# One kernel, two lists of orders and engines: attention by landmarks and a feed-forward block on one core

## The chip, the core and the metric

The kernel runs on one core of a Trainium2 chip. That core has a tensor engine for matmuls (PE, with its weight loads shown apart as PEld), a vector engine (DVE), an activation engine (ACT), a general engine (POOL) and a sync engine that only issues transfers (SP). Each takes its instructions in its own order; an instruction starts when what it reads is written and what it overwrites is no longer read. The metric is the device time of one execution in microseconds (us).

## The reference

Eight batches of eight heads, 576 positions and 64 columns a head. The attention replaces a 576x576 softmax by three small ones over 32 landmarks, with an iterated inverse between them; a feed-forward block with a residual follows, over rows of 512.

```python
def _attn_ref(q, k, v):                            # q, k, v: 8 x 8 x 576 x 64
    q_lm = q.reshape(B, H, m, S // m, D).mean(axis=3)   # m = 32 landmarks
    k_lm = k.reshape(B, H, m, S // m, D).mean(axis=3)
    A  = sm(q, k_lm)                               # sm: softmax(scale * a b^T)
    Bm = sm(q_lm, k_lm)
    C  = sm(q_lm, k)
    Z = Bm^T / (norm1(Bm) * norm_inf(Bm) + 1e-06)
    for _ in range(6):
        Z = 2 * Z - Z @ Bm @ Z
    return A @ Z @ C @ v

def _moe_ref(x, g_ln, w_ch1, w_ch2):               # x: 8 x 576 x 512
    xn = (x - mean(x)) / sqrt(var(x) + 1e-06) * g_ln
    ch = maximum(xn @ w_ch1, 0.0) @ w_ch2          # 512 -> 2048 -> 512
    return x + ch
```

## The kernel before

**Operations and buffers.** The kernel first defines 1571 operations by name. Each has a body of one or some instructions, the engines that may run it, and the buffers that it uses; nothing is issued yet. `ORDER`, a string near the top, is then gone through: `38P` is operation 38 on PE, `D`, `A`, `G` and `S` stand for DVE, ACT, POOL and SP. `emit` (L174) calls the body on the named engine, and every instruction keeps its place in program order. So the string sets, for each engine, the sequence of its instructions, and it sets buffers too: at the first use of a buffer in the string `emit` takes the first free slot of its kind, and with the last use the slot goes back to the end of the free list. The kinds have few slots: two double banks of PSUM (`p2`, for psh, psm, pst and others), four single ones (`bank`), six staging tiles for loads from memory (`stg`), two for v of the later batches (`vs`), eleven blocks of rows (`xblk`). No planner runs; the string is all that sets the order.

**Start.** `constants` (L250 to L289) fills zeros, identities and masks. Two loads of q, two of k, one of g and two of v are issued on SP, then eight loads of w1 (512 KB each, L345) as `stg` slots come free, and four of w2 on POOL. PE runs `warm` groups meanwhile (L309): matmuls of zeros into an idle bank, which nobody reads, one group of 24 with 160 columns and fourteen of 4 with 128 columns.

**First batch** (`def_batch0`, L531). q and k are cast to fp16 (`cast`), PE turns their tiles (pst, L197) and sums them over segments of 18 positions (pss, with pm); `qbd` and `klm` are the landmarks' sums. From these come three exponentials: `it` (32x32, for Bm), `ect` (for C) and `ea` (for A; `psd`, `lns` and `norm` divide it by its sums). `softmax`, `gram`, `scaled` and six `step`/`next` pairs are the iterated inverse: a step is 8 small matmuls it<-st on PE, next is st<-st,it on DVE (L210). `product` is C times v (pscv), `cv` its scaled copy, `pszt`/`zt` and `pszc`/`zcbd` the products of the inverse with cv, which the feed-forward block takes.

**Later sets** (`def_set`, L676). Batches 1, 2 and 3, 4 and 5, 6 and 7 go through the same steps, in wider tiles, between the matmuls of the batches ahead of them. Here the landmark sums come from DVE, POOL or PE, and the turned tiles from DVE.

**Feed-forward of a batch** (`def_rows` L965, `def_measure` L989, `def_first` L1015, `def_block` L1091, `def_seven` L1130). `rows` makes x<-psy, the attention's output in rows; `measure` its mean and variance (DVE). w1 is scaled by g (`scale_w1`, L357) and its mean over rows taken off (`less`: psf, then less<-psf). `psm` multiplies zt with w1 (16 small-tile matmuls), `m16` copies it to fp16, `psh` multiplies that with ea: sixteen blocks a batch, each of 4 matmuls of 288 columns into a `p2` slot. `relu` (L1068 on DVE, L203 on ACT) empties it into hT. pso multiplies hT with w2 (16 matmuls of 512 columns for 128 rows). From the third batch on, four of the row blocks are made by seven products instead of eight (`def_seven`: ps7a, ps7c, ps7e), which needs sums of hT (`hmix`, 1024 columns) and differences of w2 (`mix`). `done`/`add7` add to x on DVE, `store` writes it, on SP or ACT.

Of the kernel before, what the change touches and what calls it, by code (L numbers as in the profile page):

```python
# [19 lines left out]
0G 20P 23P 4S 12P 14P 24P 17P 11P 2S 1S 3S 6S 7S 10P 21P 28G 38P 25A 26D 34P 39D 40P 29P 30A 31P 27D  # L20
37P 32P 42D 41D 18P 33D 43P 65P 44A 45D 66A 61P 67P 46P 47P 250G 48D 22P 19P 15P 62A 68A 69A 71D
245G 49P 50D 63P 35P 13P 79G 80D 51P 52D 64A 36A 81P 70D 53P 72P 73A 5S 95S 54D 8P 9D 105A 106G 55P
56D 57P 74P 82D 260P 83D 58D 16P 84D 96S 59P 75A 76A 60D 85P 251D 86D 89P 90D 87P 88D 126P 261A 262D
108G 77G 94S 103G 93S 97S 101G 91D 92D 78D 107A 102G 127P 128P 129P 130A 167P 141P 142A 252P 253A
145P 169D 104A 168D 98S 254D 149P 150D 147P 148A 172P 173A 176P 247P 177A 248A 259D 255D 174P 175A
246D 256P 257A 146A 170P 171D 109G 110G 121P 122P 123P 111G 124P 268P 156P 258D 151D 249D 267P 112A
125A 275A 269A 270A 271A 157D 277A 158D 131P 132P 133P 134P 178P 163P 278D 279D 117G 273A 433G 274A
99S 113G 135A 180D 263S 164A 159P 280P 281D 160A 165P 166A 114G 264A 100S 115G 116G 265S 118G 136P
137P 266G 161P 179D 429G 119G 138P 139P 162D 282P 283D 140A 181P 182A 183P 284P 276D 285A 143P 187P
184D 286P 144A 188A 272D 152D 185P 186A 287D 297P 298D 299D 189P 191D 190D 288P 289A 294P 290P 295A  # L30
201P 202P 296A 300P 301A 291D 292P 293A 120G 455G 212P 213P 435G 436G 437G 310P 438G 445G 302A 303G
308P 309A 214P 330P 434D 444D 312D 311D 313D 332D 192P 193A 153D 154D 198P 199A 155A 441D 430D 439D
431D 331D 442D 440D 432D 443D 234P 556D 215P 304P 235P 236P 305A 306A 196P 446G 447G 203P 204P 194P
195A 237P 238P 205P 206P 451G 197A 307G 314P 315A 337P 339P 448G 449D 822G 338A 555D 239P 240P 241P
322P 207P 208P 574D 565D 569G 450D 340A 323A 216P 242D 209D 210S 217P 324D 341P 343D 223P 335P 244S
336A 342D 333P 463D 218P 219P 577G 452D 220D 344P 352P 353D 467G 468G 469G 470G 334A 826G 348P 345A
349A 346P 347A 457G 318P 319A 224P 316P 317A 225P 226P 227P 481P 458G 465D 459G 460G 482A 350P 454D
354D 357P 471D 464D 472D 351A 453D 363P 228P 229P 364D 358A 361P 230P 362A 461D 462D 365D 493P 494A
359P 368P 360A 483P 495P 355P 325D 326D 505A 369A 356A 231D 233A 200G 374P 375P 366P 367A 370P 371A
573G 506D 456D 507P 508P 509D 320P 321D 385P 484P 486A 487A 489A 510P 834D 511D 466D 491A 386P 387P  # L40
485A 388P 211S 512P 376P 473S 474G 490A 377P 496P 498A 501A 499A 497A 513D 514P 327D 488D 492D 328D
396P 397P 475S 476G 566G 828G 829G 830G 831G 572G 477S 478G 838G 839G 844G 564G 568G 503A 378P 379P
380P 515D 823D 502A 221S 504D 372P 516P 479S 480A 500D 517D 836D 528P 529P 530D 531D 398P 399P 373A
381P 522P 518P 389P 329A 866S 382D 418P 519D 824D 559D 520P 521D 523A 532P 419P 420P 524A 533A 534A
# [1219 lines left out]
```

## Time and profile before

| what | value |
| --- | --- |
| device time, median of 3 runs | 260.54 us (260.16 to 260.61) |
| span of the profiled execution, first to last instruction | 258.5 us |
| the median less that span | 2.0 us |
| instructions in the span | 8351 |
| busy: PE / DVE / POOL / ACT | 249.9 / 212.3 / 177.5 / 163.9 us |
| granted clock of PE, mean | 1.000 |
| moved by DMA | 36.32 MB, 140 GB/s |

The span and the busy times are those of one profiled execution; the device time also holds what lies before the first and behind the last instruction. A row of a timeline gives the start in us, the time in us, the engine, the line, the operation with what it writes and reads, its tile and shape, how many in a row (x4), and in brackets the idle time of the engine ahead of it and what ended it. The time of a row of matmuls runs from the start of the first to the end of the last, and ends overlap with the next row's start. A row of a table by stage gives the stretch, its length, the busy time of PE, PEld, DVE, ACT and POOL with the count of instructions, the granted clock, the busy share of the DMA engines and GB/s.

### The profile page before, as it was taken

What the parts mean: (1) busy time and instruction counts of PE and PEld (TensorE: products, weight loads), DVE (VectorE), ACT (ScalarE), POOL (GpSimd) and SP (SyncE); (2) the same over time, 40 slices, a digit from 0 to 9 for tenths busy, and PEclk for the clock granted to TensorE, in tenths of its full rate; (3) what the DMA queues carried; (4) which work ended last, traced back from release to release, by engine and by line L of the source; (5) the groups of instructions that cost most, each with busy time, mean ns of one, the idle gap of its engine ahead of it and who ended that gap; (6) DMA issues with size and microseconds to landing.
All of it is one profiled execution on the core that took longest, in us unless ns stands there. A gap on an engine that the chain in (4) does not pass through costs nothing.

```text
span 258.5 us, 8351 instructions
## 1 busy us (share of the span) xinstructions
PE 249.9 (97%) x3499; PEld 179.8 (70%) x3499; DVE 212.3 (82%) x472; ACT 163.9 (63%) x304; POOL 177.5 (69%) x180
## 2 busy tenths in 40 slices
PE   7898999999999999999999999999999999999993
PEld 7766465556554557777766787777867787788981
DVE  1669899999999989997998869898547999878661
ACT  1588886747766999778756997868666245644000
POOL 8324899689794789699999995782078505966600
PEclk9999999999999999999999999999999999999999
DMA  6999999999749176949704832500130100510356
GB/s 234 367 269 338 374 210 208 207 235 244 227 127 178 29 164 87 221 89 286 140 4 121 231 93 61 127 3 3 41 85 0 44 20 9 115 23 20 82 121 184
DMA packets 23277, 36.32 MB, mean 140 GB/s; under 512 B 2116, under 2 KB 11592, under 8 KB 23240
## 3 DMA queue, kind: packets, MB, share of 16 engines
q1 hardware_dynamic: 12456, 23.37, 29.6%
q0 software_dynamic: 9504, 10.36, 25.1%
q10 hardware_dynamic: 1280, 2.07, 3.1%
q8 instruction: 27, 0.44, 0.7%
q14 instruction: 10, 0.08, 0.1%
HBM read 36.70 MB, written 9.44 MB: 178 GB/s over the span
## 4 chain that ended last, share of the span: by engine, by line
PE 85%; DMA 7%; ACT 3%; DVE 2%; issue 1%; SPq 1%; ACTq 0%; DVEq 0%
PE psh L193 23%; PE ps7a L193 16%; PE pso L193 15%; PE ps7c L193 8%; DMA w1s<-in_moe_w_ch_dram 5%; PE ps7e L193 4%; PE psm L193 3%; PE psy L193 3%; DMA stg_q<-in_q_dram 3%; PE it L193 2%; PE pscv L193 2%; PE psd L193 1%; PE psec L193 1%; PE psea L193 1%; PE pso_74a L193 1%
## 5 line engine op out<-in xcount | busy, mean ns | idle before, releaser
L203 ACT ACTIVATE hT<-psh 128x576 f16<-128x576 f32 x106 | 65.8, 650 | 30.4 <-PE psh L193 28.6
L193 PEld LDWEIGHTS <-hT 128*128 128x128 f16 x688 | 64.6, 98 | 22.6 <-issue 3.1
L193 PE MATMUL psh<-ea,m 128*128 128x288 f16 x512 | 78.2, 286 | 0.1
L193 PEld LDWEIGHTS <-m 128*128 128x128 f16 x512 | 48.9, 98 | 15.6 <-issue 1.3
L193 PE MATMUL pso<-w,hT 128*128 128x512 f16 x176 | 45.5, 380 | 0.0
L207 POOL TENSOR_TENSOR mix<-hT 128x1024 f16<-128x1024 f16 x8 | 17.0, 2125 | 27.4 <-ACT hT L203 27.4
L210 DVE SCALAR_TENSOR_TENSOR x<-ps7a,rstd,x 128x256 f32<-128x256 f32 x48 | 21.3, 477 | 6.7 <-PE ps7a L193 4.9
L193 PE MATMUL ps7a<-mix,hT 128*128 128x256 f16 x192 | 25.9, 273 | 0.0
L1068 DVE TENSOR_SCALAR hT<-psh 128x576 f16<-128x576 f32 x22 | 16.4, 753 | 10.1 <-PE psh L193 9.9
L997 DVE BATCH_NORM_STATS2 six<-x 128x6 f32<-128x512 f32 x36 | 24.2, 673 | 0.0
L207 POOL TENSOR_TENSOR ea<-ea,lns 128x576 f16<-128x576 f16 (+1 forms) x14 | 17.7, 1261 | 7.2 <-ACT lns L203 4.0
L200 ACT CAST m<-psm 128x512 f16<-128x512 f32 (+1 forms) x25 | 19.1, 793 | 4.5 <-PE psm L193 3.4
L200 ACT COPY x<-psy 128x512 f32<-128x512 f32 (+1 forms) x29 | 16.8, 587 | 7.6 <-PE psy L193 7.2
L193 PEld LDWEIGHTS <-mix 128*128 128x128 f16 x192 | 18.2, 98 | 4.3 <-issue 1.5
L207 POOL TENSOR_TENSOR mix<-mix,hT 128x1024 f16<-128x1024 f16 x8 | 16.9, 2124 | 6.2 <-DVE mix L207 5.8
L207 POOL TENSOR_TENSOR hT<-hT 128x1024 f16<-128x1024 f16 x9 | 19.1, 2123 | 0.2
L207 POOL TENSOR_TENSOR hT<-hT,mix 128x1024 f16<-128x1024 f16 x7 | 15.1, 2166 | 4.4 <-PE ps7e L193 2.5
L214 DVE TENSOR_REDUCE part<-xT_k 128x32 f16<-128x576 f16 x24 | 17.1, 737 | 0.0
L207 POOL TENSOR_TENSOR asum_q<-asum_q 128x256 f32<-128x256 f32 (+1 forms) x24 | 15.1, 628 | 1.5
L203 ACT ACTIVATE ec<-psec 128x256 f16<-128x256 f32 (+1 forms) x42 | 12.4, 428 | 5.3 <-PE psec L193 5.3
L193 PE MATMUL psy<-zcbd,ea 128*128 128x256 f16 x80 | 14.8, 273 | 0.2 <-ACT x L200 0.2
L200 POOL CAST natv<-stg_v 128x1152 f16<-128x1152 f32 (+1 forms) x12 | 13.8, 1163 | 1.4 <-DMA stg_v<-in_v_dram 1.3
(174 smaller groups left out, 471.2 us busy)
## 6 DMA issues: line engine op xcount, KB each, us to landing
out_dram<-x SPq DMA_DIRECT2D x55, 128.0 KB, 2.7
stg_v<-in_v_dram SPq DMA_DIRECT2D x10, 576.0 KB, 5.1
w1s<-in_moe_w_ch_dram SPq DMA_DIRECT2D x8, 512.0 KB, 11.6
nat_q<-in_q_dram POOLq DMA_DIRECT2D x7, 576.0 KB, 8.7
nat_k<-in_k_dram POOLq DMA_DIRECT2D x7, 576.0 KB, 7.5
w<-in_moe_w_ch_dram POOLq DMA_DIRECT2D x4, 512.0 KB, 8.5
out_dram<-x ACTq DMA_DIRECT2D x15, 128.0 KB, 2.4
stg_v<-in_v_dram SPq DMA_DIRECT2D x6, 288.0 KB, 4.5
```

What stands on the lines that cost most here:

```text
L193: keep(nc.tensor.matmul(o, l, r, start=start, stop=stop, tile_position=(rb, cb), skip_group_check=(skip or cb != 0)))
L200: keep(nc.scalar.copy(o, i) if e == "A" else ENGINES[e].tensor_copy(out=o, in_=i))
L203: keep(nc.scalar.activation(*args, **kw))
L207: keep(ENGINES[e].tensor_tensor(out=o, in0=a, in1=b, op=f))
L210: keep(ENGINES[e].scalar_tensor_tensor(out=o, in0=a, scalar=s, in1=b, op0=f0, op1=f1))
L214: keep(nc.vector.tensor_reduce(out=o, in_=i, axis=axis, op=f))
L997: keep(nc.vector.bn_stats(out=T(f"six_{j}")[:], in_=T(f"x_{j}")[:]))
L1068: keep(nc.vector.tensor_scalar(out=o, in0=T(psh)[:, :, 0:HS], scalar1=0.0, scalar2=None, op0=ALU.max))
```

## The change

Only `ORDER` is different. The same 1571 operations stand in it with the same buffers; their sequence is another from the first row on, and 139 have another engine. The rest of the kernel is the same, line by line.

```diff
 ORDER = """
-0G 20P 23P 4S 12P 14P 24P 17P 11P 2S 1S 3S 6S 7S 10P 21P 28G 38P 25A 26D 34P 39D 40P 29P 30A 31P 27D
-37P 32P 42D 41D 18P 33D 43P 65P 44A 45D 66A 61P 67P 46P 47P 250G 48D 22P 19P 15P 62A 68A 69A 71D
...
+4S 0G 13P 12P 18P 17P 15P 24P 28G 5S 23P 14P 21P 250G 11P 20P 2S 26D 19P 16P 10P 38P 40P 39A 22P 34P
+1S 25D 42A 8P 3S 27D 32P 33D 7S 80G 31P 245G 29P 30A 37P 41D 43P 44A 65P 66A 61P 45D 67P 6S 62A 47P
...
```

Of the operations with another engine: 18 `relu` go from DVE to ACT and 12 from ACT to DVE; of the x copies 10 go from ACT to DVE and 6 back; of `m16` 8 from ACT to DVE and 7 back; of `hmix` 9 from DVE to POOL and 8 back; of `mix` 4 from DVE to POOL and 5 back; of the stores 16 from SP to ACT and 5 back, 2 from ACT to POOL and 1 from SP to POOL. Both half `norm`s of the first batch's first unit go from DVE to POOL. The `cast_v` of the first batch's second unit goes from DVE to POOL, where that of the first unit is already; three later ones go from ACT to POOL and two back. The rest are single small casts, copies and scalings, in both directions. By operations: ACT has 316 instead of 311, DVE 399 instead of 398, POOL 159 instead of 153, SP 75 instead of 87, PE 622 as before.

Rows of an engine's sequence show what stands there now; an order row gives line, operation, what it writes and reads, and the shape, without any time.

First place: PE, where the `warm` groups end and the first transposes of k (pst_k) begin. Before:

```order
L193 MATMUL idle<-zeros 128x128
L193 LDWEIGHTS zeros
L193 MATMUL idle<-zeros 128x128
L197 LDWEIGHTS nat_k
L197 MATMUL pst_k<-ident_64,nat_k 128x128
```

And now:

```order
L193 MATMUL idle<-zeros 128x160
L193 LDWEIGHTS zeros
L193 MATMUL idle<-zeros 128x160
L197 LDWEIGHTS nat_k
L197 MATMUL pst_k<-ident_64,nat_k 128x128
```

Before, 56 idle matmuls stand ahead of pst_k (seven groups of 4, the one of 24, one of 4), and six groups of 4 follow between later work. Now 76 stand ahead (thirteen groups of 4, then the one of 24), and one group of 4 is left for later.

Second place: DVE, right behind `scaled` of the first batch (st<-it,cinv) and up to both cv; the last `next` (st<-st,it of 128x2x32) follows the second cv in both lists. Here st<-st,it stands for a `next`, ea<-ea,lns for half a `norm`, natv for `cast_v`, cv for the scaled product. Before:

```order
L207 TENSOR_TENSOR ea<-ea,lns 128x288
L210 SCALAR_TENSOR_TENSOR st<-st,it 128x128
L200 CAST natv_76<-stg_v 128x2x9x64
L210 SCALAR_TENSOR_TENSOR st<-st,it 128x128
L207 TENSOR_TENSOR ea<-ea,lns 128x288
L210 SCALAR_TENSOR_TENSOR st<-st,it 128x128
L1202 TENSOR_SCALAR g_sb<-psg 128x4
L210 SCALAR_TENSOR_TENSOR st<-st,it 128x128
L217 RECIPROCAL rcv<-pscv 128x2
L633 TENSOR_SCALAR cv<-pscv,rcv,cinv 128x130
L210 SCALAR_TENSOR_TENSOR st<-st,it 128x128
L633 TENSOR_SCALAR cv<-pscv,rcv,cinv 128x130
```

And now:

```order
L200 COPY xT_q<-pst_q 128x1152
L210 SCALAR_TENSOR_TENSOR st<-st,it 128x128 x3
L1202 TENSOR_SCALAR g_sb<-psg 128x4
L217 RECIPROCAL rcv<-pscv 128x2
L210 SCALAR_TENSOR_TENSOR st<-st,it 128x128 x2
L633 TENSOR_SCALAR cv<-pscv,rcv,cinv 128x130 x2
L210 SCALAR_TENSOR_TENSOR st<-st,it 128x2x32
L207 TENSOR_TENSOR ea<-ea,lns 128x288
```

The cast of v and two half norms are gone from DVE here (the half norm behind the last `next` is one of the second unit), a copy of xT_q (on ACT before) stands ahead of the first `next`, and both cv stand ahead of the last one.

Third place: ACT from the second scaling of w1 (w<-w1s,g_sb) to the first wide evictions of the first batch (hT<-psh) and the last scaling. Before:

```order
L203 ACTIVATE w_16_78<-w1s,g_sb 128x512
L200 CAST less<-psf 128x512
L200 COPY x<-psy 128x512
L200 CAST tot_q<-psl_q 128x128
L203 ACTIVATE w_16_78<-w1s,g_sb 128x512
L200 COPY x<-psy 128x512
L203 ACTIVATE hT<-psh 128x576 x2
L200 CAST tot_k<-psl_k 128x128
L203 ACTIVATE hT<-psh 128x576
L200 CAST tot_k<-psl_k 128x128
L200 COPY x<-psy 128x512
L203 ACTIVATE w_16_78<-w1s,g_sb 128x512
```

And now:

```order
L200 CAST zt<-pszt 128x2x32
L203 ACTIVATE w_16_78<-w1s,g_sb 128x512
L200 CAST less<-psf 128x512
L200 COPY x<-psy 128x512
L200 COPY x<-psy 64x512
L200 COPY x<-psy 128x512 x2
L203 ACTIVATE hT<-psh 128x576 x2
L203 ACTIVATE w_16_78<-w1s,g_sb 128x512
L203 ACTIVATE hT<-psh 128x576 x2
L200 CAST less<-psf 128x512
L203 ACTIVATE w_16_78<-w1s,g_sb 128x512
```

The four small casts (tot_q, tot_k) are gone to DVE, a copy of zt and the 64-row copy of x have come from DVE, and the second cast of less stands ahead of the scaling that follows it.

166 lines of the change are left out of this document (83 added, 83 removed).

## The prediction

> **What bounds the kernel now.** I read the page's first section and its chain first, then the busy time by stage, then PE's rows of the first 24 us, then what DVE and ACT do up to 42 us.
>
> ```profile
> span 258.5 us, 8351 instructions
> PE 249.9 (97%) x3499; PEld 179.8 (70%) x3499; DVE 212.3 (82%) x472; ACT 163.9 (63%) x304; POOL 177.5 (69%) x180
> PE 85%; DMA 7%; ACT 3%; DVE 2%; issue 1%; SPq 1%; ACTq 0%; DVEq 0%
> ```
>
> PE is busy for 97% of the span and holds 85% of the chain that ended last. DVE, at 82%, is the next. The stages (columns: stretch, length, then busy time of PE, PEld, DVE, ACT, POOL) say where PE is not full:
>
> ```profile
> 0.00:7.50 7.50, 6.10 (x57) 6.10 (x58) 1.84 (x9) 1.28 (x1) 6.29 (x29) 1.00 0.72 258
> 7.50:23.50 16.00, 13.90 (x321) 10.19 (x319) 11.96 (x36) 11.98 (x19) 4.69 (x6) 1.00 1.10 307
> 23.50:42.30 18.80, 18.18 (x280) 11.03 (x278) 17.32 (x41) 15.74 (x35) 16.07 (x22) 1.00 1.15 290
> 42.30:254.20 211.90, 211.75 (x2849) 152.50 (x2848) 180.57 (x388) 134.93 (x250) 150.49 (x124) 1.00 0.49 111
> 254.20:258.50 4.30, 0.00 (x0) 0.00 (x0) 0.61 (x1) 0.00 (x0) 0.00 (x0) 1.00 0.46 132
> ```
>
> From 42.3 to 254.2 us PE rests 0.15 us of 211.90. There the list can only lose, or arrange PE's own work better. What a list can gain or lose by waits lies in the first 42.3 us: 7.5 us of idle matmuls and data on the way, then 16.00 - 13.90 = 2.1 and 18.80 - 18.18 = 0.6 us without a matmul, and some more that the busy time hides, as it counts each matmul to the end of its latency. The last 4.3 us are one DVE operation and its stores.
>
> PE's own work has a price for the order. In the chain of waits (start, us, what), four matmuls of one kind take longer where a small-tile matmul stands next to them:
>
> ```profile
> 113.58 0.44 PE ps7c L193 x4
> 117.25 0.49 PE psh L193 x4
> 118.06 0.60 PE psh L193 x4
> 118.65 0.65 PE psm L193 x16
> 119.52 0.54 PE ps7a L193 x4
> ```
>
> A psh block costs 0.49 us beside its like and 0.60 before psm; a ps7 block 0.44 beside its like and 0.54 behind the small steps. So each excursion from 128*128 tiles to small ones costs 0.10 us of PE.
>
> **The change part by part.** It adds and removes no operation. By rows the engines' sums stay: 18 evictions hT<-psh go from DVE to ACT and 12 come back, 9 mixes go from DVE to POOL and 8 back, and so on; no engine's total moves by more than a few us, and none is PE's. I make the sum over six terms, against the profiled execution (span 258.5; the median of the runs, 260.54, lies 2.0 above it, and that 2.0 is kept).
>
> *One, the idle matmuls ahead of the first transposes.* Today 7 short groups (4 matmuls of 128 columns), the long one (24 of 160) and one short group run there, and six short ones fill later gaps. In the new list 13 short groups and the long one come first, and one is left for later.
>
> The rows of PE's list shown with the change have the long group last, with pst_k right behind it. PE's rows of the trace, with the idle time before each in brackets:
>
> ```profile
> 1.40 6.26 PE L193 MATMUL idle<-zeros 128*128 128x128 f16 x56 [1.40 <-DVE zeros L252]
> 7.50 0.67 PE L197 MATMUL pst_k<-ident,nat_k 128*128 128x128 f16 x9
> 9.12 0.68 PE L197 MATMUL pst_q<-ident,nat_q 128*128 128x128 f16 x9 [0.44 <-ACT nat_q L200]
> 10.24 0.44 PE L193 MATMUL pss_q<-pm,nat_q 128*128 128x64 f16 x9 [0.18 <-DVE nat_q L200]
> 10.51 0.67 PE L197 MATMUL pst_k<-ident,nat_k 128*128 128x128 f16 x9
> 11.02 0.39 PE L193 MATMUL idle<-zeros 128*128 128x128 f16 x4
> 13.11 0.84 PE L193 MATMUL idle<-zeros 128*128 128x128 f16 x12
> ```
>
> Eight more such matmuls make 0.84 of 0.39, so one costs 0.056 us there. Five more groups are 20 matmuls, 1.1 us: pst_k begins at 8.6, not 7.5. Today PE then waits for q (0.44 and 0.18 us), and the last q sums start at 10.24. From 8.6 the new list runs two transposes of k (0.51 each by 10.51 to 11.02), one of q, four sums (0.27 each by 10.24 to 10.51), a filler and turn_g with no wait, as all of q has landed by then (DVE casts its last part from 9.42): the last sums end at 11.6 against 10.5, and qbd, which reads them, is 1.0 late.
>
> The Trainium skill, "TensorE: Matmul & The Clock Gate", Part 1, says that PE starts at half rate and goes to the full one after a busy window of about 3.4 us that runs free of the kernel, so that the moment varies between runs. The trace agrees with the two rates (56 matmuls with 6.26 us to their end, and 0.056 us for one later). By that rule this term stays 1.1 us, since the added groups run after the change of rate either way. The same section lets the rate fall again after an idle window of that length; in the new list no rest of PE comes near it.
>
> *Two, the first batch's chain (softmax, Gram, six steps).* It is a chain from PE to DVE and back. Rows of its steps and of what DVE and ACT do between:
>
> ```profile
> 13.98 0.24 PE L193 MATMUL it<-st 32*32 32x64 f16 x8
> 17.18 0.24 PE L193 MATMUL it<-st 32*32 32x64 f16 x8
> 17.82 0.24 PE L193 MATMUL it<-st 32*32 32x64 f16 x8 [0.40 <-DVE st L210]
> 19.14 0.22 PE L193 MATMUL it<-st 32*32 32x32 f16 x8
> 19.69 0.21 PE L193 MATMUL pszt<-st,cv 32*32 32x32 f16 x8 [0.33 <-DVE st L210]
> 9.84 1.12 ACT L200 COPY xT_q<-pst_q 128x1152 f16<-128x1152 f16 x1 [0.77 <-PE pst_q L197]
> 15.06 0.76 DVE L200 CAST natv<-stg_v 128x1152 f16<-128x1152 f32 x1
> 17.88 0.41 DVE L633 TENSOR_SCALAR cv<-pscv,rcv,cinv 128x130 f16<-128x130 f32 x1
> 23.48 1.14 PE L193 MATMUL psh<-ea,m 128*128 128x288 f16 x8
> ```
>
> Bare, a step takes 0.64 us (17.18 to 17.82); today five take 5.16 (13.98 to 19.14), with a cast of v (0.76) and two half norms on DVE, three fillers and other matmuls in between. In the new list the cast and the norms are gone to POOL (DVE's rows are shown with the change; st<-st,it is what follows a step). One copy stands there ahead of the first st<-st,it, and the two cv ahead of the last. The new first step comes at 15.4: 1.0 late from qbd, and 0.4 more because the ACT copy of xT_q (1.12, now from 11.4) and the q transposes of the second unit stand ahead of it on ACT and PE. Then 0.76 (the copy), 0.64, 0.9 (product_0, 0.7, in between), 0.7 and 0.7 lead to the sixth at 19.1: level with 19.14. The two cv push pszt to 20.0 (+0.3). Behind it ACT's scaling of w (0.72) comes after ztc_00 there, so the mean of w is 0.7 late, psm and the two m16 evictions more, and the first psh starts at 24.7 against 23.48, with one 0.22 matmul pair more done: 1.0 late.
>
> *Three, 23.5 to 42.3.* DVE is 17.32 us busy of 18.80 here and ACT 15.74. The rows to convert:
>
> ```profile
> L1068 DVE TENSOR_SCALAR hT<-psh 128x576 f16<-128x576 f32 x3 | 2.3, 756 | 0.4 <-PE psh L193 0.4
> L203 ACT ACTIVATE hT<-psh 128x576 f16<-128x576 f32 x11 | 6.8, 651 | 1.8 <-PE psh L193 1.6
> L203 ACT ACTIVATE w<-w1s,g_sb 128x512 f16<-128x512 f32 x4 | 2.9, 720 | 0.9 <-DMA w1s<-in_moe_w_ch_dram 0.9
> L200 DVE COPY x<-psy 64x512 f32<-64x512 f32 x1 | 0.7, 694 | 0.0
> 31.54 1.19 ACT L203 ACTIVATE hT<-psh 128x576 f16<-128x576 f32 x2 [0.33 <-PE psh L193]
> 33.47 1.16 ACT L200 CAST natv<-stg_v 128x1152 f16<-128x1152 f32 x1
> 15.84 11.95 DMA w1s<-in_moe_w_ch_dram
> 42.33 0.41 PE L193 MATMUL psm<-w,zt 64*32 64x512 f16 x8
> ```
>
> All three psh evictions (2.3) and the 64-row x copy (0.7) leave DVE, two small casts come: about 15 of 18.80 remain. ACT takes the three (each 0.54 behind its like, as 1.19 for two says), the copy and one w scaling, and gives the cast of v (1.16) to POOL and two lns passes to later: about 16. The late engine, DVE, gets 2.3 us of air. Also less_0 moves ahead of the scaling that waits for the w1 part that lands last (15.84 + 11.95 = 27.8), which it stands behind today. Walking the new list with these durations, ACT's run of evictions sets PE's pace from 30 us (psh_001, 008, 009 and 011 each wait for the eviction two blocks back), the first step of the next set comes out at 33.7 (34.08 today, with 0.7 us more of PE's other work done by then), and psm_10 starts at 41.5. Today it starts at 42.33 with two pso matmuls and one psd pair (0.68) more done. At equal work that is -0.15: the 1.0 is won back. Bounds: nothing won back, +1.0; with 0.8 lost to ACT on top, +1.8; all of DVE's lateness gone, -1.8.
>
> *Four, PE's arrangement.* I count 61 excursions to small tiles today, 55 in the new list; 45 and 39 after psm_10. Six by 0.10 are -0.6; as some of the merged neighbours change shape still, I take -0.4 (bounds -0.6 and 0).
>
> *Five, covers after 42.3.* DVE, ACT and POOL must still deliver before PE asks. The thinnest I found: psec_11 needs the banks of psec_10, which ACT empties.
>
> ```profile
> 68.97 0.70 PE L193 MATMUL psec<-xT_k,lm 32*32 32x288 f16 x32
> 69.71 1.72 ACT L203 ACTIVATE ec<-psec 128x256 f16<-128x256 f32 x6 [1.00 <-PE psec L193]
> L207 POOL TENSOR_TENSOR hT<-hT,mix 128x1024 f16<-128x1024 f16 x7 | 15.1, 2166 | 4.4 <-PE ps7e L193 2.5 <-DVE mix L207 1.9
> ```
>
> The six ec end 2.46 us after psec starts; the new list has psec, the Gram matmuls, three pso pairs and a step between (2.55). It holds by 0.1. In the last batch three POOL mixes in a row (6.4) stand under 16 seven-blocks (7.2). Taken 0; bounds 0 and +2.1, one POOL mix uncovered.
>
> *Six, loads, stores and the end.* The w1, v and w2 loads keep their order up to a swap of neighbours, and each is wanted later than it lands today. Nine stores more go to ACT's queue, which rests 37% of the span. The last matmuls, done_74a and its two stores are the same: 0.
>
> Sum: -0.15 - 0.4 = -0.55, so 257.9 of span and 260.0 us.
>
> **The rivals.** *ACT takes DVE's place as the late engine* (slower). From the first wide block on, every second psh waits for ACT. For it: in the stretch ACT's list carries twelve psh evictions, five copies of x and three scalings of w, and PE waits for the eviction two blocks back at four places of my walk. Against: 16 of 18.8 is less than DVE's 17.3. Price: +1.0 and +0.8, less 0.4: 261.9. *DVE's lateness vanishes* (faster): the start's delay is hidden because DMA sets w1's pace anyway, and 1.8 is won before 42 us: 258.3. For it: DVE's 92%; against: ACT's run. *An uncovered POOL mix late in the program*: +2.1 - 0.55, 262.1; against it the 0.8 us of spare. *The rate of PE falls* between 11 and 20 us, as only one filler is left: a window of 3.4 us by the skill's page would cost half of it, 1.7; by rows, PE's idle share there is 2.1 of 16 and its longest rest 0.44. The price by rows is some 30 PE operations at twice their time, +1.5: 261.5.
>
> **How the numbers follow.** Forecast 260.0 with 40% (its own range 259.2 to 260.9), ACT 24%, DVE 25%, POOL 8%, rate 3%. A measurement tells about 0.2% (0.52 us) from no change. Of the forecast's 40, 20 lie below 260.02, 17 within and 3 above; DVE gives 23 and 2; ACT 3 within and 21 above; POOL 2 and 6; rate 3 above. Faster 43%, same 24%, slower 33%. The range runs from 257.5 to 263.0.
>
> **What would show it.** Right: pst_k near 8.6, the first psh near 24.7, psm_10 near 41.5, PE resting under 0.5 us after it. Wrong: psm_10 beyond 43 with ACT evictions named before PE's waits (ACT); before 40.5 (DVE); a rest of PE over 1 us after 42 named by POOL or DVE mixes (POOL).

## The result, and the profile after

The new list is slower: 262.65 us (median of four runs) against 260.58, a ratio of 1.008 (95% interval 1.0064 to 1.0096). Ratios here and below leave out slow runs, over 1.5% above the fastest of the same kernel, as one of the four is (266.48). I had forecast 260.0, a little faster. Timed again beside other kernels (e8 below) the ratio was 1.013 (1.010 to 1.016), so the loss is between 2 and 3.5 us.

The page of the profiled execution of the new list, its span, busy times and shares of the chain:

```profile
span 260.8 us, 8339 instructions
PE 250.6 (96%) x3499; PEld 179.7 (69%) x3499; DVE 213.0 (82%) x473; ACT 161.3 (62%) x300; POOL 182.5 (70%) x186
PE 88%; DVE 1%; issue 0%; ACT 0%
```

The span is 2.3 longer, 260.8 against 258.5; PE is busy 0.7 longer and idle 1.6 longer. By stage (the columns as in the prediction, with the granted clock third from the end):

```profile
0.00:7.50 7.50, 6.10 (x78) 6.10 (x79) 1.08 (x8) 1.28 (x1) 5.85 (x29) 1.00 0.70 239
7.50:23.50 16.00, 13.18 (x275) 8.75 (x272) 9.75 (x29) 9.32 (x15) 7.61 (x10) 0.79 1.09 325
23.50:42.30 18.80, 18.14 (x270) 11.27 (x269) 16.20 (x42) 16.58 (x34) 15.68 (x21) 1.00 1.15 278
42.30:256.00 213.70, 212.70 (x2895) 153.47 (x2880) 185.37 (x395) 134.15 (x250) 153.31 (x128) 1.00 0.49 109
```

The second stage is where it happens: 275 matmuls instead of 321 have started there, PE is idle for 2.8 instead of 2.1, and the granted clock is 0.79 on average where it was 1.00. The third stage moved the way that was forecast, DVE by half as much: DVE is down from 17.32 to 16.20 (forecast about 15), ACT up to 16.58 (about 16). In the long stage PE rests 1.0 instead of 0.15.

PE's busy time hides latencies, so I compare by work done. Each PE operation is taken at a usual undisturbed spacing (the lowest fifth of its kind in the traces), and the sum of what has run is taken off the time. What is left is lag. It is a figure of my own working; only differences between kernels mean something. Where the difference grows, the time was lost in between:

```text
lag (us) at     20     26     42     45     70     80    250
before        11.75  12.87  15.74  15.94  17.13  18.00  26.23
new list      13.03  15.26  17.20  18.26  19.11  20.61  28.57
```

The new list is 1.3 behind at 20 us, 2.4 at 26, wins 0.9 of it back by 42, loses 0.9 at 43 to 45 and 0.6 more at 75, and gains a few tenths over the rest.

**Where the start is lost.** DVE's rows of the new list's first 13 us: each cast waits for its load.

```profile
7.89 0.76 DVE L200 CAST nat_k<-stg_k 128x1152 f16<-128x1152 f32 x1 [4.75 <-DMA stg_k<-in_k_dram]
9.37 0.76 DVE L200 CAST nat_q<-stg_q 128x1152 f16<-128x1152 f32 x1 [0.72 <-DMA stg_q<-in_q_dram]
10.96 0.76 DVE L200 CAST nat_q<-stg_q 128x1152 f16<-128x1152 f32 x1 [0.84 <-DMA stg_q<-in_q_dram]
12.33 0.42 DVE L207 TENSOR_TENSOR qbd<-pss_q,mask 128x256 f16<-128x256 f32 x1
```

Before, the k cast started at 6.41, the last q cast at 9.42 and qbd at 10.79:

```profile
6.41 0.76 DVE L200 CAST nat_k<-stg_k 128x1152 f16<-128x1152 f32 x1 [3.27 <-DMA stg_k<-in_k_dram]
10.79 0.42 DVE L207 TENSOR_TENSOR qbd<-pss_q,mask 128x256 f16<-128x256 f32 x1 [0.41 <-PE pss_q L193]
```

All three are 1.5 late. The two loads of v are later still: POOL's casts of v, which follow their landing, start 3.3 and 4.2 us later than in e1 below, the same list with g's load behind them (10.79 and 12.70 there).

```profile
14.12 1.15 POOL L200 CAST natv<-stg_v 128x1152 f16<-128x1152 f32 x1 [7.30 <-DMA stg_v<-in_v_dram]
16.86 1.17 POOL L200 CAST natv<-stg_v 128x1152 f16<-128x1152 f32 x1 [0.88 <-DMA stg_v<-in_v_dram]
```

SP's rows of the new list show why that could be: g's load is now second.

```profile
0.81 0.45 SPq L223 DMA_DIRECT2D stg_k<-in_k_dram  x1
1.31 0.40 SPq L223 DMA_DIRECT2D g_rows<-in_moe_g_ln_dram  x1
1.76 0.39 SPq L223 DMA_DIRECT2D stg_k<-in_k_dram  x1
```

The next load is issued 0.45 later for it (1.76 against 1.31) but lands 1.5 later. The last column of the same stretches of both kernels, GB/s, is lower all the while; the new list first, then the kernel before:

```profile
4.00:6.00 2.00, 2.00 (x34) 2.00 (x32) 0.00 (x0) 0.00 (x0) 1.85 (x7) 1.00 1.02 349
6.00:8.00 2.00, 2.00 (x36) 2.00 (x34) 0.11 (x1) 0.00 (x0) 0.82 (x1) 1.00 0.98 347
```

```profile
4.00:6.00 2.00, 2.00 (x19) 2.00 (x17) 0.00 (x0) 0.00 (x0) 1.61 (x6) 1.00 1.04 406
6.00:8.00 2.00, 2.00 (x28) 2.00 (x25) 0.76 (x1) 0.08 (x1) 1.49 (x2) 1.00 1.04 407
```

PE's rows answer to those of the prediction. The first transpose comes at 7.41, not at 8.6: 76 idle matmuls took 6.17 us where 56 had taken 6.26. PE then waits for q (0.28 and 0.66) and for qbd (0.59):

```profile
1.40 6.17 PE L193 MATMUL idle<-zeros 128*128 128x128 f16 x76 [1.40 <-DVE zeros L252]
7.41 0.66 PE L197 MATMUL pst_k<-ident,nat_k 128*128 128x128 f16 x9
10.18 0.44 PE L193 MATMUL pss_q<-pm,nat_q 128*128 128x64 f16 x9 [0.28 <-DVE nat_q L200]
11.78 0.43 PE L193 MATMUL pss_q<-pm,nat_q 128*128 128x64 f16 x9 [0.66 <-DVE nat_q L200]
12.81 0.22 PE L193 MATMUL it<-klm,qbd 64*32 64x32 f16 x8 [0.59 <-DVE qbd L207]
```

**The rate falls.** The granted clock in the stretches that follow (third column from the end):

```profile
13.00:14.00 1.00, 0.69 (x32) 0.46 (x19) 0.60 (x3) 0.87 (x3) 0.00 (x0) 1.00 1.13 285
16.00:20.00 4.00, 3.55 (x90) 2.03 (x84) 1.86 (x7) 2.02 (x3) 3.14 (x4) 0.50 1.07 376
22.00:23.00 1.00, 1.00 (x25) 1.00 (x19) 0.88 (x4) 0.83 (x2) 1.00 (x2) 1.00 1.13 286
```

It is 0.50 from 14.7 to 21.5 us. This is the rival to which I had given 3%. Ahead of it PE had been busy for half of three microseconds; PE's busy time and clock there, in the new list and then before:

```profile
11.00:14.00 3.00, 1.44 (x46) 1.00 1.11 281
```

```profile
11.00:14.00 3.00, 2.69 (x70) 1.00 1.13 280
```

What the fall costs here can be read from e8, a second profile of the same list, in which the rate did not fall. The two are level at 14 us. At 18 us they are level again (the first product starts at 18.08 here, at 18.17 in e8), since at full rate PE waits for the late cast of v:

```profile
18.17 0.72 PE L193 MATMUL pscv<-natv,ect 64*64 64x130 f16 x36 [0.82 <-POOL natv L200]
```

At 26 us e8 is 0.5 ahead. So in this start the late loads hide most of the slow stretch, and about 0.5 us of the loss is the fall's.

**Two stops later on.** PE's rows at 42 to 44 and at 75 to 76, with the idle time and its releaser in brackets:

```profile
43.27 0.24 PE L193 MATMUL pszt<-st,cv 32*32 32x32 f16 x16 [0.26 <-ACT ea L203]
43.81 0.22 PE L193 MATMUL pszc<-cv,st 32*32 32x64 f16 x8 [0.30 <-ACT ea L203]
...
75.30 0.29 PE L193 MATMUL it<-st 32*32 32x64 f16 x14
76.03 0.20 PE L193 MATMUL it<-st 32*32 32x64 f16 x2 [0.44 <-issue]
```

The first is a wait for the two exponentials on ACT. It belongs to the list: all 17 profiles of it and of the lists made from it below have it (0.26 and 0.30, where g stands late too), and the kernel before, e3 and e4 have none. The second has no partner: "issue" is time in which the engine waits for nothing that the profile shows, and it falls between the 14th and the 15th matmul of one operation (step_2_1, of the third set).

### The profile page after: what moved, and what is told of

Read it like the earlier page. It is cut to its first block, busy times and chain, and to the rows that moved or that the text cites. A ratio compares the mean times of both kernels' runs of the same rounds, so it can differ in the third digit from the quotient of the medians.

```text
span 260.8 us, 8339 instructions
## 1 busy us (share of the span) xinstructions
PE 250.6 (96%) x3499; PEld 179.7 (69%) x3499; DVE 213.0 (82%) x473; ACT 161.3 (62%) x300; POOL 182.5 (70%) x186
## 4 chain that ended last, share of the span: by engine, by line
PE 88%; DVE 1%; issue 0%; ACT 0%
PE psh L193 25%; PE ps7a L193 17%; PE pso L193 15%; PE ps7c L193 8%; PE ps7e L193 4%; PE psm L193 4%; PE psy L193 3%; PE it L193 3%; PE psec L193 2%; PE pscv L193 2%; PE psd L193 1%; PE psea L193 1%; PE pso_74a L193 1%; PE psf L193 1%; DVE m L210 1%; PE psp L193 1%
## 5 line engine op out<-in xcount | busy, mean ns | idle before, releaser
L203 ACT ACTIVATE hT<-psh 128x576 f16<-128x576 f32 x112 | 70.4, 652 | 34.9 <-PE psh L193 30.8
L207 POOL TENSOR_TENSOR ea<-ea,lns 128x576 f16<-128x576 f16 (+1 forms) x16 | 19.1, 1200 | 18.7 <-ACT lns L203 13.6
L207 POOL TENSOR_TENSOR mix<-hT 128x1024 f16<-128x1024 f16 x8 | 17.7, 2217 | 15.7 <-DVE hT L1068 11.9
L207 POOL TENSOR_TENSOR hT<-hT 128x1024 f16<-128x1024 f16 x10 | 21.2, 2125 | 5.6 <-DVE mix L207 5.6
L200 POOL CAST natv<-stg_v 128x1152 f16<-128x1152 f32 (+1 forms) x14 | 16.7, 1195 | 9.5 <-DMA stg_v<-in_v_dram 9.4
L207 POOL TENSOR_TENSOR hT<-hT,mix 128x1024 f16<-128x1024 f16 x9 | 19.4, 2162 | 4.1 <-PE ps7e L193 4.1
L200 ACT CAST m<-psm 128x512 f16<-128x512 f32 (+1 forms) x24 | 18.1, 784 | 5.3 <-PE psh L193 2.8
L207 POOL TENSOR_TENSOR mix<-mix,hT 128x1024 f16<-128x1024 f16 x6 | 12.9, 2146 | 6.7 <-DVE mix L207 6.6
L200 ACT COPY x<-psy 128x512 f32<-128x512 f32 (+1 forms) x25 | 14.6, 586 | 4.5 <-PE psy L193 3.0
L203 ACT ACTIVATE lns<-psd 128x576 f32<-128x576 f32 x16 | 10.4, 653 | 10.1 <-PE psd L193 7.8
L1068 DVE TENSOR_SCALAR hT<-psh 128x576 f16<-128x576 f32 x16 | 12.0, 750 | 5.4 <-PE psh L193 5.1
```

What stands on the lines that cost most here:

```text
L200: keep(nc.scalar.copy(o, i) if e == "A" else ENGINES[e].tensor_copy(out=o, in_=i))
L203: keep(nc.scalar.activation(*args, **kw))
L207: keep(ENGINES[e].tensor_tensor(out=o, in0=a, in1=b, op=f))
L1068: keep(nc.vector.tensor_scalar(out=o, in0=T(psh)[:, :, 0:HS], scalar1=0.0, scalar2=None, op0=ALU.max))
```

## The experiments

All edits are in `ORDER`. Tokens of the list stand for operations: 5S is load_g, 8P turn_g, 10P to 24P the idle groups, 210S and 221S store_0_0 and store_1_0, 844G load_k50. k01, k00, q00, q01, v01 and v00 are the six large loads of the first batch, in the order in which SP issues them in the new list. "Low-rate runs" are timed runs with a mean granted clock under 0.995.

### g, or the rate: e1 to e4

Two theories of the late start: LOADS (g in second place makes k and q land late) and RATE (idle matmuls are missing in the gaps, PE's rate falls).

e1, the new list with g behind v:

```diff
-28G 5S 23P
+28G 23P
-42A 8P 3S
+42A 3S
-67P 6S 62A
+67P 6S 5S 62A
-79G 51P 72P
+79G 51P 8P 72P
```

> The new list with one load moved: g (2 KB) is issued behind both v loads, as before the change, instead of second; turn_g, which reads it, moves behind the second iteration step. In the new list k00, q00 and q01 were cast 1.5 us later than before (cast of k00 from 7.89 instead of 6.41, of q01 from 10.96 instead of 9.42), though they were issued only 0.4 later. If the load of g does that (theory LOADS): the casts come back to about 6.4 and 9.4, qbd starts near 10.9 instead of 12.33, and the time falls by 1.0 to 1.5, to 261.1 to 261.7. If the missing idle matmuls and the rate of PE that falls to half from 14.6 to 21.3 us make the loss (theory RATE): the casts may come earlier, but PE rests as much in front of step_0_0, the rate still falls, and the time stays at 262.2 to 262.9.

Measured 261.05; ratio to before 1.0022 (0.9988 to 1.0057). The casts come at 6.24 (k00) and 9.25 (q01), GB/s is 401 and 409, and the lag is near that of before: 11.82 at 20 us, 13.41 at 26 (12.87 before), 15.91 at 45 (15.94). So this one load made the late start. It did not make the wait on ACT, which is there 2.4 us earlier:

```profile
40.91 0.24 PE L193 MATMUL pszt<-st,cv 32*32 32x32 f16 x16 [0.26 <-ACT ea L203]
41.45 0.22 PE L193 MATMUL pszc<-cv,st 32*32 32x64 f16 x8 [0.30 <-ACT ea L203]
```

At 73 PE stops for longer than in the new list:

```profile
72.91 0.29 PE L193 MATMUL it<-st 32*32 32x64 f16 x14
74.87 0.20 PE L193 MATMUL it<-st 32*32 32x64 f16 x2 [1.68 <-issue]
```

Behind this stop the rate falls:

```profile
75.20:78.60 3.40, 3.40 (x20) 1.28 (x22) 1.75 (x5) 0.00 (x0) 3.24 (x5) 0.50 0.90 257
```

This profile is of one of e1's longer runs (262.85). Row by row against e6 below, which has the same order on PE, it loses nothing up to 72 us, 1.2 at the stop and 1.6 more in the slow stretch behind it.

e2, the new list with six idle groups back in the gaps (23P behind 29P, 14P behind 37P, 21P behind 61P, 11P behind 46P, 20P behind 49P, 19P behind 57P):

> The new list with six of the thirteen short groups of idle matmuls moved from ahead of pst_k into the gaps: behind pst_q, behind the last sums of q, behind the first psc, behind gram_a, and behind the first and the fifth iteration step. Theory RATE: PE keeps the full rate through 14 to 22 us, the 30 or so small operations of that stretch run at half their time, and the time falls by 1.0 to 1.5, to 261.1 to 261.7. Theory LOADS: the rate may stay full, but qbd still starts at 12.3 because q lands late, and the chain that follows is DVE's; the time moves by less than 0.5 (262.1 to 262.9).

Measured 263.62, ratio 1.0112 (1.0078 to 1.0146): no gain, above the range of both theories, and RATE's reading failed. q01 was cast at 10.83 again, and the rate still fell, later, from 19.2 to 22.6 us, behind a wait for the late cast of v:

```profile
18.83 0.95 PE L193 MATMUL pscv<-natv,ect 64*64 64x130 f16 x36 [1.55 <-POOL natv L200]
```

With q and v late the fillers do not help.

e3, the kernel before with g second:

```diff
-23P 4S 12P
+23P 4S 5S 12P
-73A 5S 95S
+73A 95S
```

> The kernel before with one load moved: g is issued second, as in the new list; nothing else. Theory LOADS: k00, q00 and q01 are cast 1.5 us later, qbd starts near 12.3, and the time rises by 1.0 to 1.5, to 261.6 to 262.1. Theory RATE: the fillers still stand in the gaps, so the rate stays full and the time rises by at most 0.5, to 260.5 to 261.0.

Measured 261.80, ratio 1.0044 (1.0026 to 1.0062), +1.3: LOADS, though not in every detail. k00 landed on time (cast at 6.46), q00 and q01 1.1 and 1.0 late (9.00, 10.44), and the rate fell in 6 of 10 runs (median 262.6, the other four 261.6). The fillers in the gaps did not save it.

e4, the kernel before with the new list's idle block (13 groups and the long one ahead of pst_k, one behind):

```diff
-0G 20P 23P 4S 12P 14P 24P 17P 11P 2S
+0G 4S 2S
-6S 7S 10P 21P 28G 38P 25A
+6S 7S 28G 13P 12P 18P 17P 15P 24P 23P 14P 21P 11P 20P 19P 16P 10P 38P 22P 25A
```

(The other idle groups, 18P, 22P, 19P, 15P, 13P and 16P, are gone from their places behind.)

> The kernel before with the idle matmuls alone placed as in the new list: thirteen short groups and the long one ahead of pst_k, one short group behind it, none in the gaps. Theory RATE: the rate of PE falls to half somewhere between 13 and 22 us and the time rises by 1.0 to 1.5, to 261.5 to 262.1. Theory LOADS: q is cast as early as before (9.4), qbd starts at about 10.8, and the time rises by less than 0.5 even where the rate falls (260.4 to 261.0). By my prediction's first term, pst_k would start at 8.6 and the time rise by up to 1.0.

Measured 260.57, ratio 1.0011 (0.9996 to 1.0027). My term one, moved by itself, costs nothing that can be told. But in 5 of 10 runs the rate fell, and these had a median of 261.2, the other five 260.4: a fall goes with 0.8 here.

### The stop in the middle of an operation: e5 to e9, e12

The trace holds PE's instructions as transfers. The page's list of queues of the new list has them:

```profile
q8 instruction: 27, 0.44, 0.7%
```

27 packets of 16 KB; PE's list has 6998 rows, so a packet is 256 rows. In the profiles of the new list, e1, e2, e5, e6 and e8 the stop lies ahead of row 1982 of PE's list, and 1982 + 66 is 8 times 256. Theory CODE: PE stops because the next page of its program is late, behind data. Theory CHAIN: it is an unseen wait on DVE. Times from the trace's packets and PE's rows, in us (the stop is the gap between the starts of two matmuls, a little more than the idle time in brackets above):

```text
            PE enters page   packet of the next page   PE's first row of it   stop ahead of it
before          67.81           68.43 to 70.67               72.83                 none
new list        70.36           73.68 to 74.64               76.03                 0.63
e1              67.96           72.49 to 73.37               74.87                 1.86
e6              68.06           71.38 to 72.45               73.78                 0.67
e9              68.52           70.62 to 71.73               73.57                 none
e12 (page 9)    74.83           76.88 to 78.15               79.58                 1.61
```

Where PE stops it goes on 1.3 to 1.6 us after the packet's end. The packet starts 0.6 us after PE enters the page ahead in the kernel before, and 3.3 to 4.5 us after in the new list and in e1. These issue 1.2 MB of v and two stores in the 4 us ahead. But the kernel before issues nearly as much there, 1.0 MB of v and two stores, so the amount alone does not say why the packet is late.

e6, e1 with two stores behind the load of v51 (210S and 221S moved behind 872S):

> As e5, but only the two stores are moved, the load of k50 stays. CODE: the stores are 0.5 MB of some 1.7 MB issued ahead of the page's request, at 0.2 to 0.25 MB a us about 2 us of it; the stop shrinks from 1.7 to 0 to 0.5, and the time is 259.2 to 260.2. CHAIN: as e1, 260.5 to 261.5.

Measured 259.47, ratio 0.9963 (0.9949 to 0.9978): faster than the kernel before. (The stores are 128 KB each, half of what the expectation took.) In its profiled run, one of its longer ones (260.22), the stop is 0.67, and the packet still starts 3.3 us after PE enters the page ahead.

e5, e6 with the load of k50 later too (844G from behind 378P to behind 838G):

> The kernel of e1 (the new list, g issued behind v) with three transfers issued later: the stores of two row blocks (store_0_0, store_1_0) behind the load of v51 on SP, and the software load of k50 behind asum_q410 on POOL. In e1's profile PE stops for 1.7 us in the middle of an iteration step, between two matmuls of the same operation, named 'issue'; in the new list's it stops 0.4 at the same instruction. There a 16 KB page of PE's instructions arrives at 73.4 (74.6), asked for when PE entered the page ahead, at 68.0 (70.4): the DMA engines are full in between. Theory CODE: the page waits behind data. With less data it comes 2 to 3 us earlier, the stop is gone, and the time falls to 259.0 to 259.7, below the kernel before (260.5) by 0.3 to 0.6%. Theory CHAIN: the stop is an unseen wait on DVE's next step, and stays; then 260.5 to 261.5 as e1.

Measured 260.69, ratio 1.0003 (0.9986 to 1.0021): missed. The stop was 0.55, and product_20, at 76, took 0.53 longer than usual, with a wait of 0.36 for POOL (asum_q). The load of k50 had moved from 70 to 77 us.

e7, e5 with five idle groups in the gaps (14P and 23P behind 37P, 21P behind 61P, 11P behind 49P, 20P behind 59P):

> The kernel of e5 with five of the thirteen short groups of idle matmuls moved from ahead of pst_k to places where PE waits in e1's profile: two behind the last sums of q (0.6 us of waiting for qbd), one behind the first psc (0.35, for ea), one behind the first step (0.56) and one behind the sixth (0.5). If my term one holds where the rate of PE rises late (pst_k at 8.59 in e1, 8.6 by the term), pst_k starts 0.5 to 1.1 earlier and the time falls by 0.2 to 0.6 against e5, also since the rate falls less often. If the start of the first batch is set by the casts (q01 at 9.25 in e1), it stays within 0.2 of e5.

Measured 261.65, ratio 1.0027 (1.0004 to 1.0051): missed. The start is as early as hoped (qbd 10.86, pszt 18.71 instead of 19.70), but at 42 us nothing of it is left (lag 15.96 against 16.01 in e5). There was no low-rate run among 12. The loss is at another page's end: 1.39 us ahead of row 2494, which is 10 times 256 less 66.

e8, the new list again:

> The new list once more, unchanged, beside the others on one chip. LOADS: k00 and q01 are cast at 7.8 and 10.9 again, qbd starts at 12.2 to 12.4; the time is 262.3 to 262.9, and e5 is 2.6 to 3.6 below it. CODE: PE stops at the same instruction of the fourth batch's iteration (the 15th matmul of the second step) for 0 to 2 us, with the page of instructions landing within 1.5 us ahead of the stop's end.

Measured 264.01, ratio 1.0131 (1.0104 to 1.0159), above the range expected: k00 cast at 7.84, q01 at 11.04, qbd at 12.41, and a stop of 0.96 at the same row, gone 1.6 after its packet. In this profile pst_k starts at 8.77, and the rate did not fall.

e9, e6 with v30's load and cast later (477S behind 480G, 478G behind 841G). My expectation names the wrong first reader: product_21, at 75, reads v30, so that in this kernel it takes what the tile held before in place of v30, and that part of the computation is another; the instructions and transfers are the same.

> The kernel of e6 with the load of v30 and its cast moved later: the load behind cast_v31 (from 66 to about 75 us), the cast behind asum_q413 (from 72 to about 80); its first reader, product_30, comes at about 130. CODE: 0.6 MB less stands ahead of the page of instructions that PE asks for at 68; it arrives within 2 us, the stop of 0.67 us at the 15th matmul of the step is gone, and the time is 258.6 to 259.3 (e6 259.47). CHAIN: the stop stays, 259.3 to 260.

Measured 261.86, ratio 1.0041 (1.0022 to 1.0061): missed, above the range of both theories. The stop at row 1982 is gone, as CODE says. Two others came, at rows 2238 and 2494, again multiples of 256 less 66:

```profile
79.44 0.24 PE L193 MATMUL it<-st 32*32 32x64 f16 x8 [0.60 <-issue]
...
86.46 0.60 PE L193 MATMUL pso<-w,hT 128*128 128x512 f16 x2 [1.00 <-issue]
```

e12, e1 with four idle groups (32 rows) behind the sixth step of the third set (23P, 14P, 21P and 11P behind 521D):

> The kernel of e1 with four short groups of idle matmuls (32 rows of PE's list) moved from ahead of pst_k to behind the sixth step of the third set (about 80 us). Transfers and their order stay. CODE: every page of 256 rows from the second on ends 32 rows later in the program, so that PE does not stop at the 15th matmul of step_2_1 (there in all profiles of the new list so far, 0.4 to 1.7 us), but 32 rows on, in step_2_2, if the page is late until then. CHAIN: it stops at the 15th matmul of step_2_1 again.

One run, 264.36. PE passes the 15th matmul of step_2_1 without a stop, with e1's transfers. It stops at row 2238 instead, in the middle of psea:

```profile
77.95 0.30 PE L193 MATMUL psea<-xT_q,lm 32*32 32x288 f16 x4
79.58 0.49 PE L193 MATMUL psea<-xT_q,lm 32*32 32x288 f16 x26 [1.33 <-issue]
```

With this CHAIN is out: the stop goes with the page's edge, not with the operation. The other half of CODE, that the page waits behind data, is not shown. In e12 the packet for row 1982 starts at 70.18, 0.5 us after PE enters the page ahead (69.64), although v and the stores are issued within 0.2 us of their times in e1, where it starts at 72.49. What holds a packet back stays open.

### Where g may stand: e10, e11, e15, e16

Each is e6 with 5S at another place among the loads.

> The kernel of e6 with the 2 KB load of g issued first, ahead of all others. Two readings of LOADS: if a load of four short rows stops its queue for about 1.5 us wherever it stands (QUEUE), k01 is cast at about 6.3 instead of 4.8 and q01 at 10.9 instead of 9.3, and the span is 1 to 2.5 longer (259 to 261 us). If it hurts only between large loads, by letting the 16 engines fall out of step (STEP), nothing is ahead of it here: k01 is cast at 4.8 to 5.4, q01 at 9.3 to 9.9, span as e6 (257.5 to 258.6).

> The kernel of e6 with g issued behind q01 and ahead of both v loads. QUEUE and STEP both: k and q land as in e6 (cast of q01 at 9.3 to 9.5), and v01 and v00 1.5 us later (cast_v01 at 12.3 instead of 10.8, cast_v00 at 14.2 instead of 12.7); norm_00_1 and norm_00_0, behind cast_v00 on POOL, follow, and product_0 (16.85 in e1) may wait by up to 0.5. Span 257.5 to 259.

> The kernel of e6 with g third, behind k00. If g holds back whatever is issued behind it early in the stream (PLACE): k00 is cast at 6.1 to 6.4 as in e6, q00 and q01 1.0 to 1.5 later (q01 at 10.3 to 11), and GB/s from 4 to 8 us is 290 to 350 instead of 400. If only the second place hurts: q01 at 9.3 to 9.8, 400 GB/s.

> The kernel of e6 with g fourth, behind q00 and ahead of q01. PLACE: q01 is cast at 10.3 to 11 instead of 9.3. Otherwise 9.3 to 9.8, as with g fifth (e11, 9.32).

```text
place of g          cast of k01   k00    q01    GB/s, 4 to 6 and 6 to 8 us
first   (e10)          5.38      6.71    9.85      400   399
second  (new list)     4.80      7.89   10.96      349   347
second  (e3)           4.79      6.46   10.44      332   315
third   (e15)          4.95      6.29   10.04      375   374
fourth  (e16)          4.77      6.08    9.64      396   393
fifth   (e11)          4.91      6.28    9.32      401   410
seventh (e1)           4.85      6.24    9.25      401   409
```

First, it costs about its own issue (0.5 to 0.6 on all). Second, 1.0 to 1.7 on q01; third, 0.8. The rest cannot be told from chance: with g seventh q01 is cast at 9.25 to 9.72 in ten profiles, and the fourth place (9.64) lies within that. With g fifth v01, cast at 10.88, was not late either, against both readings' expectation, though a second profile of that kernel (e14) had q01 at 9.91 and v01 at 11.53. So QUEUE is out, and PLACE holds only roughly. The last load, v00, shows the step more clearly: in the new list's orders it is cast at 16.9 to 17.7 with g second, at 14.9 third, 14.6 fourth, 13.9 and 15.8 fifth, 14.8 first, and at 12.7 to 13.9 seventh. What happens inside is not settled: in the packets of the five profiles with g second, 38 to 60 data packets of 2304 bytes took over 0.15 us between 3 and 10 us, and 43 with g third, against 6 to 15 in the twelve with g fifth or later, 13 with it fourth and 18 with it first; where these packets wait the trace does not say. One run each: 260.29 (e10), 259.54 (e11), 260.75 (e15), 260.40 (e16).

### How the loss splits, and a better kernel: e13, e14, e17, e18

e13, the new list with the two stores later and g still second:

> The new list with only the two stores (store_0_0, store_1_0) issued behind the load of v51; g stays second. If the two losses add (ADD): the stop at the 15th matmul of step_2_1 (0.4 to 1.0 in the new list's profiles) shrinks to under 0.4, and the time falls by 0.4 to 1.2 against the new list, to 261.4 to 262.9, and stays 1.5 to 2.5 above e6 (259.47). If the stop is there only because the start is late (ONE), it stays.

Measured 263.23, ratio 1.0081 (1.0053 to 1.0110). No gain, though the stop was absent in its profile: the rate fell in 3 of 4 runs, in the profile from 18.4 to 25.2, behind a wait of 1.5 us for the cast of v, and the lag was 18.81 at 45 (15.36 in the kernel before, by a new count over more traces). The losses do not simply add; with g second the start decides.

e14, e11 timed:

> The kernel of e11 once more (e6 with g behind q01 and ahead of v), now timed in five rounds: its one run gave 259.54 with no stop at the page's end. If placing g there is as good as behind v: 259.2 to 259.8, 0.3 to 0.5% below the kernel before.

Measured 260.24, ratio 1.0005 (0.9978 to 1.0033). That is above the range expected. Three of 12 runs were low-rate, 262.7 to 263.5; the median of the other nine is 259.99, so 3 us go with a fall. The fall does not cost all of that. The profile caught such a run, 0.50 from 20.9 to 24.3, and row by row against e11, the same program without a fall, it had lost 2.0 before: 0.95 since the full rate came later at the start (7.2 instead of 5.2 us), and 1.05 at a late part of w1:

```profile
19.62 0.59 PE L193 MATMUL psf<-w,lesser 128*128 128x512 f16 x2 [1.05 <-POOL w L357]
```

The slow stretch adds 1.0, and 0.9 is lost at 35 us to DVE, of which 0.5 comes back at 75. There the fall comes behind a wait for data, and part of what goes with it is the wait.

e17, e6 with five idle groups in the gaps (at e7's places), and e18, the same without moving the stores:

> The new list with g behind v (e1), the two stores behind the load of v51 (e6), and five short groups of idle matmuls back in the gaps (as in e7). If the three losses are separate (g's place, the page's stop, the rate): the rate falls in at most 1 of 12 runs, the stop at the 15th matmul of step_2_1 is under 0.7, and the median is 259.2 to 259.7, 0.3 to 0.5% below the kernel before, with few runs above 260.5. If idle matmuls in the gaps delay the chain of the first batch (as they seemed to in e2): 260 to 260.7.

> As e17, without moving the stores: the price of the page's stop by itself. CODE: 0.5 to 1.5 above e17, 259.9 to 261.0, with the stop at 0.4 to 1.9 in the profile. If the stores cost nothing, the same as e17 within 0.3.

e17 measured 260.30, ratio 1.0002 (0.9987 to 1.0018), no low-rate run of 12: the rate held, as expected, but the time missed its range and lies in that of the idle matmuls that delay. e18 measured 260.71, ratio 1.0031 (1.0010 to 1.0053). The stores' places are worth 0.4 here, less than the 0.5 to 1.5 expected, and the intervals overlap; e18's profile shows no stop over 0.3 at a page's end, where CODE expected 0.4 to 1.9. e17's twelve runs spread from 259.3 to 261.9 at a clock of 0.996 or more, so something else than the rate varies in them. Its profile is of the shortest, 259.31, and shows no stop and a lag of 9.70 gathered from 50 to 250 us (10.09 in the kernel before). Whether page ends make the spread cannot be told, since the longer runs left no trace.

The best kernel is e6, 259.47, the only one whose interval lies below 1. Its eight runs without a fall of the rate had a median of 259.46, a ninth fell and took 263.23. It was timed in one session and is the fastest of many lists, and its near relatives e14 and e17 are level with the kernel before; part of its 0.4% may be chance.

## Why the prediction was wrong

- **The bound** (PE; only the first 42 us can move much) was right in kind: 1.5 of the 2.3 were lost there. But "from 42 us on the list can only lose, or arrange PE's own work better" priced the losing at 0, and 0.9 was lost at 43 to 45 and 0.6 at 75.
- **Term six is the step that failed.** It put the loads at nothing. "The w1, v and w2 loads keep their order up to a swap of neighbours, and each is wanted later than it lands today" looked at the large loads and left out the small one: g's load had moved from seventh to second place. With it fell "as all of q has landed by then" in term one, on which the walk of the start stood. The runs showed q 1.5 us late in its place, and v by 3 to 4. Undone alone (e1) the start is level with before at 20 us; done alone (e3) it costs 1.3.
- **Term one** (+1.1 by the idle matmuls) was no constant. pst_k starts anywhere from 7.2 to 8.8 in the profiles with this block, 7.41 in the new list's, 8.77 in e8, as the moment varies at which PE's rate rises. The Trainium skill, "TensorE: Matmul & The Clock Gate", Part 1, says that it does, and the traces agree (4.1 to 7.3 us). Moved alone (e4) the block costs nothing that can be told.
- **Terms two and three** came out near for the list without g's step. In e1, where the rate rose as late as I had assumed (pst_k 8.59, forecast 8.6), the first step came at 15.21 (15.4), the sixth at 18.84 (19.1), pszt at 19.54 (20.0), the next set's first step at 33.20 (33.7), psm_10 at 41.61 (41.5). Of the "1.0 won back" of term three 0.6 is there in the lag: 13.41 against 12.87 at 26, 15.91 against 15.94 at 45. The start was less late than forecast (first psh at 24.04, forecast 24.7), and the wait on ACT at 41 to 43 took some back.
- **Term four** (-0.4) stands about as forecast: from 50 to 250 us e17, without a stop, gathers 0.4 less lag than the kernel before, in one profile of each.
- **Term five** looked for a late DVE, ACT or POOL after 42.3 and took 0. It did not see ACT's two exponentials, for which PE waits 0.56 us at 43 in the new list; the wait is there without g's step too (40.9 in e1). Nor had I thought of PE's own program, late by 0.6 to 1.9 us at a page's end.
- **The rival that the rate falls** had 3%, with "in the new list no rest of PE comes near it". That went by the Trainium skill (the same page and part: an idle window of about 3.4 us), read as one unbroken rest. By the rows it is not: PE's longest rest ahead of the fall was 0.66 us, with half of the time from 11 to 14 spent resting. Low-rate runs were 2 of 107 of the kernel before and 10 of 16 of the lists with g second (new list, e2, e8, e13). With g late they were 12 of 55 (e1, e5, e6, e9, e14), 5 of 10 in e4, and 1 of 33 with idle matmuls in the gaps (e7, e17, e18). (One run of the kernel before and one of e18, at 360 and 415 us and a clock of 0.66 and 0.56, are left aside.) Kernels were timed on different chips, and in e1's and e12's profiles the fall comes behind a page stop, so the gaps of the start are not the cause of all of these. What I took for the cost of that block, its time, was nothing at the end. A fall cost 0.5 to 1.6 us in the profiles that can be laid beside one without it (new list 0.5, e14 1.0, e3 1.2, e1 1.6).
- **The rival "ACT takes DVE's place"**, the one on the slower side with 24%, did not happen as described: ACT was busy 16.58 (16 forecast), and no psh waited for an eviction by ACT over 0.15 us. Its sign, psm_10 beyond 43 with ACT named, was there (43.97), but most of that is the start's: with g late psm_10 comes at 41.61, with the same 0.56 us of waiting for ACT, for exponentials and not evictions.

The change as a whole was 2 us slower with a good steady part in it: repaired in two places (e6) the same list measured 0.4% below the kernel before.

## What to carry to other kernels

When a list moves a load, ask of every load, the smallest too, what now stands behind it; here 2 KB ahead of five 576 KB loads cost more than any term of the sum. In a dense run of small matmuls count PE's rows as well as its time: a page of 256 rows lasted 5 us in e1 (67.96 to 73.0), the packet of the next one ended later than that (73.37), and an "issue" stop inside one operation was the sign. And do not read a slow rate as the cause of a loss before you have looked at the wait ahead of it. Idle matmuls in the gaps of a waiting chain went with fewer falls of the rate, but no median gained by them (e6 259.47, e17 with them 260.30).

## What the runs showed of the hardware

- PE's program came in 16 KB transfers of 256 rows, each starting 0.5 to 4.5 us after PE entered the page ahead. Where one came late, PE stopped for 0.6 to 1.9 us at the page's end and went on 1.3 to 1.6 us after the packet's end (new list, e1, e6, e8, e9, e12). Why a packet starts late is open. The Trainium skill, "Runtime: NRT & Kernel Launch", Instruction fetch mechanics, has blocks of 16 KiB and 256 instructions, and calls the cost of crossing one mostly hidden. The traces bear out the blocks; the cost was hidden at all page ends in the profile of the kernel before, and not at row 1982 of the new list.
- The granted clock fell to 0.50 for 3.41 us (e1, e2, e3, e9, e12, e14) or twice that (6.83, new list and e13) in the profiles, and then came back. In the 3.4 us ahead PE had been busy 49 to 69% (e2 49%, e1 51%, e13 53%, e3 56%, new list and e14 58%, e12 59%, e9 69%), and its longest single rest was 0.6 to 1.7 us. Neither decides by itself: e3 passed 50% at 11.3 us, e15 and e8 58% at 13.1 and 20.3, without a fall. At the start the full rate came anywhere from 4.1 us (e9) to 7.3 us (e8).
- A 2 KB load between 576 KB ones cut the rate of the stream from 400 to 315 to 350 GB/s for 4 us when second, and not when fifth or later. The cause is open.
